# The rotor block's first two angle products moved in beside the gated block's last token sums

## The chip, the cores and the metric

The kernel runs on one core of one Trainium2 chip. The metric is the device time of one execution in microseconds, median of several. Three runs of the kernel before gave 814.88 us in the median (814.73 to 819.56).

## The reference, cut to what matters

Three blocks follow one another; the change lies where the second hands over to the third.

```python
x = attn(...)                       # (4, 768, 384): recurrent delta-rule attention
# gated block
h = np.maximum(x @ w_in, 0.0)       # u, v = halves of 512 columns
v_n = (v - mu) / np.sqrt(var + 1e-06)
v_s = np.einsum('ts,bsd->btd', w_spatial, v_n) + b_spatial[None, :, None]
x = (u * v_s) @ w_out
# rotor block
theta = x @ w_theta
zr, zi = x * np.cos(theta), x * np.sin(theta)
y = np.einsum('ts,bsd->btd', w_tok_r, zr) + np.einsum('ts,bsd->btd', w_tok_i, zi)
u = x + y
out = u + np.maximum(u @ w_ch, 0.0)
```

## The kernel before, in words

Every step is a task with a priority, the engines that can do it and the tiles it reads and writes (`Plan.add`, L152). While the program is built, a list scheduler (`Plan.run`, L237) takes the tasks one by one: for an engine, the ready task of the lowest priority number. The order in which it takes them is the fixed order of each engine's queue on the chip; a queue does not overtake. SP's queue issues all the DMAs.

A float32 product is made from three products of split operands (high·high, high·low, low·high), 128 rows at a time; `split` (L892) makes the two halves with a cast (ScalarE or VectorE) and a subtraction (VectorE or GpSimd).

The gated block, per batch b of 4, for each of 6 tiles of 128 tokens: `m_T` loads x transposed, `m_V` makes v and its layer norm, `m_U` makes u. Then six token sums `m_S` (L1058), 36 matmuls of 256 columns each; VectorE evicts each sum (L1069), multiplies it by u (L1072), and SP stores it. Those of the last batch have the priorities 1090 to 1095.

The rotor block, for 24 tiles (b, i): `X2` (L1227, 12 matmuls) is the product with w_out, evicted to tile x; `T2` (L1238) transposes it, with three evictions (xh, xl, x2T); `TH` (L1257, 9 matmuls) is the product with w_theta, followed by range reduction (ni, two steps of rr, a clamp), Sin, Abs, Sin of the rest, two products with x, and two splits into z. `Y` (L1285) adds the tile's part of the token sums, 36 matmuls into six PSUM banks y that are held for the whole batch: 18 with w_tok_r and z from the cosine, 18 with w_tok_i and z from the sine. After the sixth tile, `U2` and `O` finish the batch. The order that the priorities give is: X2 and T2 of tiles 0 and 1 at 1092.5 (XP, L54), TH of tiles 0 and 1 at 2004 and 2005, and then for each n: X2 and T2 of tile n+2 (2010 + 10n), Y of tile n (2013 + 10n), TH of tile n+2 (2013.5 + 10n).

PSUM: X2, T2, TH, the gated block's products and O share two banks m (`r_m`, L520). The six banks y are free from the end of the attention on.

SBUF: pools open and close. `ta` (L1150) opens p2a and the banks y once the attention is done. `tb` (L1160) closes the gated block's pools pm and wi and opens p2 once every task of the gated block is done, but for its last stores. In p2 lie all tiles of TH behind its product (ni, rr, sn, cs, z), the token weights of tiles 1 to 5, and the four buffers cvm3 (L1171) through which these weights are loaded from DRAM (L1179) before they are split. w_tok_i goes into the ring w3 (`r_wsp`, L899) that holds the gated block's token weights, a place at a time as those are done with. TH's matmuls wait for tb too.

Of the kernel before, what the change touches and what calls it, by code (L numbers as in the profile page):

```python
# [23 lines left out]
DM = H * D  # L24
# [5 lines left out]
TG = 256  # L30
# [20 lines left out]
THD = 1.5  # L51
LOADLAT = 2900
M3 = 4
XP = 1092.5  # L54
PMP = .5
PER = 6
HAMW = 4096 / 1.2
# [64 lines left out]
        return self.pools[self.pool].tile(self.shape, self.dtype, tag=self.tag, name=self.tag, bufs=self.bufs)  # L122


class Task:
    __slots__ = ("opts", "fn", "deps", "prio", "extra", "crit", "users", "left", "eng", "start", "end", "allocs", "uid", "big", "act", "credit", "order", "banks", "port", "part", "mode")

# [10 lines left out]
class Plan:  # L138
# [13 lines left out]
    def add(self, opts, fn, reads=(), writes=(), prio=0.0, extra=0.0, crit=False, after=(), big=False, act=0.292,  # L152
            port=True, part=0, mode=1):
        t = Task()


        t.port, t.part, t.mode = port, part, 0 if big else mode
        t.big, t.act, t.credit = big, 0.98 if big else act, 0.0
        t.opts, t.fn, t.prio, t.extra, t.crit = opts, fn, prio, extra, crit
        t.deps, t.users, t.allocs, t.eng, t.order = set(after), [], [], None, set()  # L160
        t.uid = len(self.tasks)
        t.banks = [b for b in reads if b.psum or b.ring is not None and b.ring.pool[:2] == "ps"]
        for b in reads:
            t.deps.update(b.writers)
            b.readers.append(t)
        for w in writes:
            b, part = w if isinstance(w, tuple) else (w, False)
            if not part:
                t.deps.update(b.readers)
                t.deps.update(b.writers)  # L170
            if b.first is None:
                b.first = t
                if b.ring is not None:
                    t.allocs.append(b)
            elif b.first is not t:
                t.order.add(b.first)
            b.writers.append(t)
        t.deps.discard(t)
        self.tasks.append(t)
        return t  # L180
# [234 lines left out]
def kernel(  # L415
# [34 lines left out]
    def ring(pl, tag, shape, dtype=F32, bufs=1):  # L450
        return Ring(pools, pl, shape, dtype, tag, bufs)
# [19 lines left out]
    def o_dve(n):  # L471
        return [("DVE", d_dve(n))]
# [21 lines left out]

    pool("const")
    pool("w3")
    pool("wi")
    pool("pm")
    pool("dram", space=bass.MemoryType.DRAM)
# [410 lines left out]
    r_wsr = Ring(pools, "w3", [128, HALF], F32, "gt", 2)  # L910
    r_gt = ring("w3", "gt", [128, 2, TG], F32, 2)
    r_wsr.items = r_gt.items
    r_xTh = ring("pm", "xTh", [128, KX, TG], F32R, 2)
    r_xTl = ring("pm", "xTl", [128, KX, TG], F32R, 2)
    r_uT = ring("pm", "uT", [128, KF, TG], F32, 3)
    r_hv = ring("pm", "hv", [128, DF], F32, HVN)
    r_st = ring("pm", "st", [128, 6], F32, 2)
# [195 lines left out]
                m_S(b, h3, fp, pr)  # L1113
                pr += 1

    r_bgr = ring("pm", "bgr", [128, BGW, 2], I32, 2)
    r_bgm = ring("pm", "bgm", [128, BGW], F32, 2)
    wdram = {}

    bg0 = [marks[BG0]]  # L1120
# [78 lines left out]
    r_x2T = ring("p2a", "x2T", [128, KX, S], F32, 2)  # L1199
    r_xh = ring("p2a", "xh", [128, KX, 128], F32R, 2)  # L1200
    r_xl = ring("p2a", "xl", [128, KX, 128], F32R, 2)
    r_ni = ring("p2", "ni", [128, DM], I32, 1)
    r_rr = ring("p2", "rr", [128, DM], F32, 2)
    r_sn = ring("p2", "sn", [128, DM], F32, 2)
    r_cs = ring("p2", "cs", [128, DM], F32, 2)
    r_z = [ring("p2", f"z{i}", [128, DM], F32R, 2) for i in range(4)]
    r_uf = ring("p2", "uf", [128, HALF], F32, 8)
    r_uh = ring("p2", "uh", [128, HALF], F32R, 4)
    r_ul = ring("p2", "ul", [128, HALF], F32R, 4)
    r_hp = ring("p2", "hpi", [128, 1], F32, 1)  # L1210
    hpi = r_hp.new()
    P.add([("POOL", 100.0)], lambda e: nc.gpsimd.memset(hpi.t, TWO_PI / 4), [], [hpi], 1900.0, port=False)
    sw = ring("p2a", "sw", [128, 1], F32, 1).new()
    P.add([("POOL", 100.0)], lambda e: nc.gpsimd.memset(sw.t, 0.0), [], [sw], 900.0, port=False)
    P.add([("ACT", 1500.0)], lambda e: act(sw.t, sw.t, ACTF.Sin), [], [sw], 903.0, after=sqrts)
# [3 lines left out]
    def load_g(b, h3, pr):  # L1219
        gh, gl = r_gh.new(), r_gl.new()  # L1220
        g_b[b, h3] = (gh, gl)
        for f in range(KF // 2):
            raw, gd = r_gr.new(), gdram[b][f][h3]
            P.add(dma(262144), lambda e, raw=raw, gd=gd: nc.sync.dma_start(out=raw.t, in_=gd.t), [gd], [raw], pr, extra=LOADLAT)
            split(raw, lambda raw=raw: raw.t, 2 * TG, gh, lambda f=f: gh.t[:, 2 * f:2 * f + 2], gl, lambda f=f: gl.t[:, 2 * f:2 * f + 2], pr)

    def X2(b, i, pr):  # L1227
        h3, o = i // 2, (i % 2) * 128
        if i % 2 == 0:
            load_g(b, h3, pr - 40 if pr >= 2000 else 903.0)  # L1230
        gh, gl = g_b[b, h3]
        ps, x2 = r_m.new(), r_x2.new()
        x2_b[b, i] = x2
        gr = [lambda f=f: (gh.t[:, f, o:o + 128], gl.t[:, f, o:o + 128], wo_h[f].t, wo_l[f].t) for f in range(KF)]
        mm_tasks(ps, lambda: ps.t[:, 0:DM], gr, DM, [[gh, gl, wo_h[f], wo_l[f]] for f in range(KF)], pr)
        P.add(o_cpp(DM), lambda e: copy(e, x2.t, ps.t[:, 0:DM]), [ps], [x2], pr, port=False)

    def T2(b, i, pr):  # L1238
        if i == 0:
            x2T_b[b] = [r_x2T.new()]  # L1240
        x2, ps, xT = x2_b[b, i], r_m.new(), x2T_b[b][0]
        xh, xl = xhl[b, i] = r_xh.new(), r_xl.new()
        v3 = (lambda: ps.t[:, 0:384].rearrange("p (k t) -> p k t", k=KX))

        def f(e):
            for kk in range(KX):
                nc.tensor.transpose(v3()[:, kk, :], x2.t[:, kk * 128:(kk + 1) * 128], ident.t)

        t = P.add(o_pe(245), f, [x2, ident], [ps, xh, xl], pr, act=0.95, mode=0)
        t.order.add(mfifo[-1])  # L1250
        mfifo.append(t)
        P.add([("ACT", d_actp(384))], lambda e: copy(e, xh.t, v3()), [ps], [xh], pr)
        P.add(o_dve(384), lambda e: nc.vector.tensor_tensor(out=xl.t, in0=v3(), in1=xh.t.bitcast(F32), op=ALU.subtract),
              [ps, xh], [xl], pr, port=False)
        P.add(o_cpp(384), lambda e: copy(e, xT.t[:, :, i * 128:(i + 1) * 128], v3()), [ps], [(xT, True)], pr, port=False)

    def TH(b, i, pr):  # L1257
        xh, xl = xhl[b, i]
        x2, ps = x2_b[b, i], r_m.new()
        gr = [lambda kk=kk: (xh.t[:, kk], xl.t[:, kk], wt_h[kk].t, wt_l[kk].t) for kk in range(KX)]  # L1260
        n1 = len(P.tasks)
        mm_tasks(ps, lambda: ps.t[:, 0:DM], gr, DM, [[xh, xl, wt_h[kk], wt_l[kk]] for kk in range(KX)], pr)
        for t in P.tasks[n1:]:
            t.deps.add(tb)
        ni, rr, sn, cs = r_ni.new(), r_rr.new(), r_sn.new(), r_cs.new()
        th = (lambda: ps.t[:, 0:DM])
        P.add(o_dve(DM), lambda e: nc.vector.tensor_scalar(out=ni.t, in0=th(), scalar1=1.0 / TWO_PI, scalar2=None, op0=ALU.mult),  # L1267
              [ps], [ni], pr, port=False)
        P.add(o_dve(DM), lambda e: nc.vector.scalar_tensor_tensor(out=rr.t, in0=ni.t, scalar=-C1, in1=th(), op0=ALU.mult, op1=ALU.add),  # L1269
              [ps, ni], [rr], pr, port=False)  # L1270
        P.add(o_dve(DM), lambda e: nc.vector.scalar_tensor_tensor(out=rr.t, in0=ni.t, scalar=-C2, in1=rr.t, op0=ALU.mult, op1=ALU.add),
              [ni], [rr], pr)
        P.add([("DVE", d_dve2(DM)), ("POOL", 1456.0)],
              lambda e: eng[e].tensor_scalar(out=rr.t, in0=rr.t, scalar1=PI_F, scalar2=-PI_F, op0=ALU.min, op1=ALU.max),
              [], [rr], pr)
        P.add([("ACT", d_acts(DM))], lambda e: act(sn.t, rr.t, ACTF.Sin), [rr], [sn], pr)
        P.add([("ACT", d_acts(DM))], lambda e: act(rr.t, rr.t, ACTF.Abs), [], [rr], pr)
        P.add([("ACT", d_acts(DM) + 93)], lambda e: act(cs.t, rr.t, ACTF.Sin, bias=hpi.t, scale=-1.0), [rr, hpi], [cs], pr)
        z = z_b[b, i] = [r.new() for r in r_z]
        for q, src in ((0, cs), (2, sn)):  # L1280
            P.add(o_tts(DM), lambda e, src=src: eng[e].tensor_tensor(out=src.t, in0=x2.t, in1=src.t, op=ALU.mult),
                  [x2], [src], pr)
            split(src, lambda src=src: src.t, DM, z[q], lambda q=q: z[q].t, z[q + 1], lambda q=q: z[q + 1].t, pr, part=False)

    def Y(b, i, pr):  # L1285
        z = z_b[b, i]
        for h3 in range(2):
            for q, (wh, wl) in ((0, (wr_h, wr_l)), (2, (wm_h, wm_l))):
                for d in range(KX):
                    if i == 0 and q == 0:  # L1290
                        y_b[b, d, h3] = r_y2[d][h3].new()
                    y = y_b[b, d, h3]
                    t0, t1 = h3 * HALF, (h3 + 1) * HALF
                    d0, d1 = d * 128, (d + 1) * 128
                    gr = [lambda q=q, wh=wh, wl=wl, t0=t0, t1=t1, d0=d0, d1=d1:
                          (z[q].t[:, d0:d1], z[q + 1].t[:, d0:d1], wh[i].t[:, t0:t1], wl[i].t[:, t0:t1])]
                    mm_tasks(y, lambda y=y: y.t, gr, HALF, [z[q], z[q + 1], wh[i], wl[i]], pr,
                             start=(i == 0 and q == 0), stop=(i == NT - 1 and q == 2))
# [27 lines left out]
    T2(*seq[0], XP + 0.1)  # L1326
    X2(*seq[1], XP + 0.2)
    T2(*seq[1], XP + 0.3)
    TH(*seq[0], pr + 4)
    TH(*seq[1], pr + 5)  # L1330
    for n, (b, i) in enumerate(seq):
        pr += 10
        if n + 2 < len(seq):
# [70 lines left out]
```

## Time and profile before

| | us |
|---|---|
| median of three runs | 814.88 (814.73 to 819.56) |
| profiled execution, device time | 812.64 |
| span of that execution, first to last instruction | 810.9 |
| TensorE busy in it | 750.0 |

The times quoted from the trace are microseconds from the span's start in the profiled execution. TensorE's matmuls are pipelined: the duration shown of one is longer than the distance to the next. The granted clock is a share of 2.4 GHz.

### The profile page before, as it was taken

Reading aid. Unit: us, or ns where it says so; the run is one execution under the profiler, and the core shown is the slowest. Engines: PE = TensorE matmul, PEld = TensorE weight load, DVE = VectorE, ACT = ScalarE, POOL = GpSimd, SP = SyncE. Lnnn points to the kernel's source line nnn. Section 1 sums busy time; section 2 is a strip of 40 time slices with the busy share of each in tenths; the row PEclk is TensorE's granted clock in tenths of the full one; section 3 lists DMA queues with packets and bytes.
Section 4 is the critical chain, followed back from the end, with each engine's and each line's share of the span. In section 5 each row is a group of like instructions: output and inputs, shape, how many; then the busy total and the mean of one; then the engine's idle time right before and its main releaser. Section 6 shows DMA issues by size and latency. Waiting matters only on the chain.

```text
span 810.9 us, 21951 instructions
## 1 busy us (share of the span) xinstructions
PE 750.0 (92%) x8904; PEld 685.8 (85%) x8904; DVE 623.9 (77%) x1537; ACT 342.5 (42%) x766; POOL 159.0 (20%) x178
## 2 busy tenths in 40 slices
PE   5389879989999989999999999889999999999998
PEld 5377658778987767888879999889999999999997
DVE  5989998999998999999775573787565575556545
ACT  4636326536444454534653351354333342333321
POOL 2026612543122241302011000131111111111100
PEclk9999989999999989999999999989999999999999
DMA  7626625454577887487884601451010011002001
GB/s 226 210 62 187 175 79 149 128 165 135 176 233 211 236 231 216 147 234 245 214 253 130 211 2 40 133 151 41 20 72 27 27 37 62 25 24 75 1 1 59
DMA packets 84997, 102.43 MB, mean 126 GB/s; under 512 B 8992, under 2 KB 65568, under 8 KB 84896
## 3 DMA queue, kind: packets, MB, share of 16 engines
q1 hardware_dynamic: 84896, 101.03, 42.1%
q8 instruction: 70, 1.15, 0.6%
q14 instruction: 31, 0.25, 0.1%
HBM read 74.38 MB, written 22.41 MB: 119 GB/s over the span
## 4 chain that ended last, share of the span: by engine, by line
PE 61%; DVE 26%; DMA 5%; issue 4%; ACT 2%; SPq 1%; POOL 1%; POOLq 0%; DVEq 0%; ACTq 0%
PE m L961 30%; PE y L961 19%; DVE un L721 5%; DVE tmp L709 5%; PE mg L486 2%; PE gp L651 2%; PE ru L832 1%; DVE kq L779 1%; PE py L860 1%; DVE un L687 1%; DVE bgm L886 1%; PE ru L821 1%; DMA kg<-in_kqT_dram 1%; PE s L848 1%; DVE GX L662 1%
## 5 line engine op out<-in xcount | busy, mean ns | idle before, releaser
L961 PE MATMUL m<-w,vh 128*128 128x256 f32 x576 | 110.3, 291 | 0.7 <-ACT uT L454 0.7
L961 PEld LDWEIGHTS m<-w,vh 128*128 128x128 f32 x576 | 89.0, 191 | 4.2 <-ACT uT L454 1.1
L961 PE MATMUL y<-wr,z 128*128 128x384 f32 x432 | 88.1, 343 | 0.0
L961 PE MATMUL y<-w,z 128*128 128x384 f32 x432 | 84.6, 339 | 0.0
L961 PE MATMUL m<-w,vl 128*128 128x256 f32 x288 | 81.5, 283 | 0.8 <-POOL vl L895 0.5
L961 PEld LDWEIGHTS y<-wr,z 128*128 128x128 f32 x432 | 77.3, 191 | 0.0
L961 PEld LDWEIGHTS y<-w,z 128*128 128x128 f32 x432 | 75.6, 188 | 0.0
L721 DVE TENSOR_TENSOR un<-un,tmp 128x30 f32<-128x30 f32 (+21 forms) x209 | 70.2, 348 | 1.1
L709 DVE TENSOR_TENSOR tmp<-un 128x30 f32<-128x30 f32 (+21 forms) x209 | 67.9, 337 | 1.2
L1267 DVE TENSOR_SCALAR ni<-m 128x384 int32<-128x384 f32 x24 | 13.3, 556 | 58.8 <-PE m L961 58.8
L961 PEld LDWEIGHTS m<-w,vl 128*128 128x128 f32 x288 | 54.9, 191 | 1.2 <-POOL vl L895 0.7
L961 PE MATMUL m<-wo,gh 128*128 128x384 f32 x192 | 48.9, 335 | 1.6 <-DVE rr L1269 1.6
L961 PE MATMUL m<-xTh,wih 128*128 128x256 f32 x144 | 46.3, 322 | 0.0
L454 ACT ACTIVATE W<-ru 64x192 f32<-64x192 f32 x88 | 28.5, 324 | 41.4 <-PE ru L833 40.1
L454 ACT ACTIVATE x<-m 128x384 f32<-128x384 f32 x15 | 7.3, 488 | 87.5 <-PE m L961 87.5
L629 POOL TENSOR_TENSOR gm<-mask,ng 128x256 f32<-128x256 f32 x53 | 36.4, 690 | 38.8 <-DVE pp L672 17.0
L797 POOL TENSOR_TENSOR vk<-vk,ng 128x384 f32<-128x384 f32 x25 | 23.7, 946 | 95.9 <-DMA vk<-in_vkn_dram 47.0
L486 PE MATMUL mg<-ident 128*128 128x128 f32 x231 | 39.6, 310 | 3.0 <-ACT GX L454 1.4
L832 PEld LDWEIGHTS ru<-rt,GX 64*64 64x64 f32 x384 | 26.2, 136 | 18.6 <-DVE rt L825 14.7
L832 PE MATMUL ru<-rt,GX 64*64 64x48 f32 x384 | 32.2, 224 | 10.0 <-DVE rt L825 9.4
L961 PE MATMUL m<-xTl,wih 128*128 128x256 f32 x144 | 40.6, 282 | 0.0
L961 PE MATMUL m<-xTh,wil 128*128 128x256 f32 x144 | 40.5, 281 | 0.0
(192 smaller groups left out, 2090.6 us busy)
## 6 DMA issues: line engine op xcount, KB each, us to landing
kq<-in_kqT_dram SPq DMA_DIRECT2D x96, 128.0 KB, 3.9
vk<-in_vkn_dram SPq DMA_DIRECT2D x48, 192.0 KB, 3.9
kg<-in_kqT_dram SPq DMA_DIRECT2D x32, 256.0 KB, 3.5
gd<-gt SPq DMA_DIRECT2D x24, 256.0 KB, 2.5
graw<-gd SPq DMA_DIRECT2D x24, 256.0 KB, 2.8
k<-in_vkn_dram SPq DMA_DIRECT2D x24, 192.0 KB, 3.2
xd<-xs SPq DMA_DIRECT2D x48, 96.0 KB, 3.2
xr<-xd SPq DMA_DIRECT2D x24, 192.0 KB, 3.5
```

The source lines that it names most:

```text
L454: nc.scalar.activation(out=out, in_=in_, func=func, **kw)
L486: nc.tensor.transpose(MGt[:, 256:384], ident.t, ident.t)
L629: eng[e].tensor_tensor(out=gm.t, in0=mask.t.unsqueeze(1).to_broadcast([128, HP, CH]), in1=ng_b[r].t[:, j, 1].unsqueeze(2).to_broadcast([12 ...
L651: mm(out=pv()[o:o + 64, hp, :], lhsT=kh, rhs=kg.t[i:i + D, :, hp, :] if fused else kh, start=True, stop=True)
L662: nc.vector.scalar_tensor_tensor(out=GXt[1][:, u0 + hp], in0=GXt[1][:, u0 + hp], scalar=ng_b[1].t[:, j, 1, hp:hp + 1], in1=mask.t, op0=ALU ...
L687: nc.vector.transpose(out=un.t, in_=gx[:, :, 0:32].rearrange("p u t -> p t u"))
L709: eng[e].tensor_tensor(out=t3, in0=un.t[:, k:k + 1, 0:k].to_broadcast([128, m, k]), in1=un.t[:, t0:32:st, k:k + 1].to_broadcast([128, m, k ...
L721: eng[e].tensor_tensor(out=un.t[:, t0:32:st, 0:k], in0=un.t[:, t0:32:st, 0:k], in1=t3, op=ALU.add)
L797: lambda e: eng[e].tensor_tensor(out=vk.t, in0=vk.t, in1=ng_b[r].t[:, j].unsqueeze(3).to_broadcast([128, 2, HP, D]), op=ALU.mult), [ng_b[r ...
L832: mm(out=pu.t[64:128, hp, :], lhsT=gx[64:128, u, :], rhs=rt.t[64:128, hp, :], start=True, stop=True)
L961: mm(out=view(), lhsT=a, rhs=c, start=(start and q == 0 and s_ == 0), stop=(stop and q == tot - 1 and s_ == 2))
L1267: P.add(o_dve(DM), lambda e: nc.vector.tensor_scalar(out=ni.t, in0=th(), scalar1=1.0 / TWO_PI, scalar2=None, op0=ALU.mult), [ps], [ni], pr ...
```

## The change

It makes TH of tiles 0 and 1 independent of tb and gives it an early priority.

- A new pool pz, which is never closed, takes four rings out of pm: xTh and xTl (the transposed x of the gated block) and bgr and bgm (buffers in which weights were converted during the attention). TH's tiles become later users of these places (`again`): rr takes bgm's; sn and cs are the two halves of bgr's; the four z are halves of xTh's and xTl's. ni lies on sn. There are two of each, as before (ni had one). p2's rings for them are gone.
- X2, T2 and TH of tiles 0 and 1 write into the six banks y, which are empty then (`bank`), in place of m.
- Their TH no longer waits for tb. Its priorities are 1092.5 and 1093.0 (TP) in place of 2004 and 2005; X2 and T2 move from 1092.5 to 1091.5 (XP).
- The constant hpi lies in p2a and is written early.
- Y of tile 0 does its 18 cosine matmuls first and then its 18 sine matmuls; before, the two alternated in nines.

```diff
-XP = 1092.5
+XP = 1091.5
+TP = (1092.5, 1093.0)
...
+    pool("pz")
...
-    r_xTh = ring("pm", "xTh", [128, KX, TG], F32R, 2)
-    r_xTl = ring("pm", "xTl", [128, KX, TG], F32R, 2)
+    r_xTh = ring("pz", "xTh", [128, KX, TG], F32R, 2)
+    r_xTl = ring("pz", "xTl", [128, KX, TG], F32R, 2)
...
-    r_bgr = ring("pm", "bgr", [128, BGW, 2], I32, 2)
-    r_bgm = ring("pm", "bgm", [128, BGW], F32, 2)
+    r_bgr = ring("pz", "bgr", [128, BGW, 2], I32, 2)
+    r_bgm = ring("pz", "bgm", [128, BGW], F32, 2)
...
-    r_ni = ring("p2", "ni", [128, DM], I32, 1)
-    r_rr = ring("p2", "rr", [128, DM], F32, 2)
-    r_sn = ring("p2", "sn", [128, DM], F32, 2)
-    r_cs = ring("p2", "cs", [128, DM], F32, 2)
-    r_z = [ring("p2", f"z{i}", [128, DM], F32R, 2) for i in range(4)]
+
+    def again(r, shape, dtype):
+        n = Ring(pools, r.pool, shape, dtype, r.tag, r.bufs)
+        n.items = r.items
+        return n
+
+    r_rr = again(r_bgm, [128, DM], F32)
+    r_sc = again(r_bgr, [128, 2, DM], F32)
+    r_zc, r_zs = again(r_xTh, [128, 2, DM], F32R), again(r_xTl, [128, 2, DM], F32R)
...
+    def bank(b, i, k):
+
+        return r_m.new() if b or i > 1 else r_y2[k][i].new()
+
...
-        ps, x2 = r_m.new(), r_x2.new()
+        ps, x2 = bank(b, i, 0), r_x2.new()
...
-        x2, ps, xT = x2_b[b, i], r_m.new(), x2T_b[b][0]
+        x2, ps, xT = x2_b[b, i], bank(b, i, 1), x2T_b[b][0]
...
-        x2, ps = x2_b[b, i], r_m.new()
+        x2, ps = x2_b[b, i], bank(b, i, 2)
...
-        for t in P.tasks[n1:]:
-            t.deps.add(tb)
-        ni, rr, sn, cs = r_ni.new(), r_rr.new(), r_sn.new(), r_cs.new()
+        if b or i > 1:
+            for t in P.tasks[n1:]:
+                t.deps.add(tb)
+        rr, sc = r_rr.new(), r_sc.new()
+        sn, cs = Half(sc, 0), Half(sc, 1)
+        ni = sn
...
-        z = z_b[b, i] = [r.new() for r in r_z]
+        z = z_b[b, i] = [Half(w, q) for w in (r_zc.new(), r_zs.new()) for q in range(2)]
...
-        for h3 in range(2):
-            for q, (wh, wl) in ((0, (wr_h, wr_l)), (2, (wm_h, wm_l))):
+        hq = [(h3, q) for h3 in range(2) for q in (0, 2)]
+        for h3, q in sorted(hq, key=lambda x: x[::-1]) if (b, i) == (0, 0) else hq:
+            for wh, wl in ((wm_h, wm_l) if q else (wr_h, wr_l),):
...
-    TH(*seq[0], pr + 4)
-    TH(*seq[1], pr + 5)
+    TH(*seq[0], TP[0])
+    TH(*seq[1], TP[1])
```

## Rows read from the trace of the kernel before

**Rows 1.** The page's head: the span and the instructions in it

```profile
span 810.9 us, 21951 instructions
```

**Rows 2.** Waits of TensorE from 440 us on, the longest: total, times, longest one

```profile
PE m L961 <- ACT xh L454: 2.6, 1, 2.6
PE m L1247 <- ACT x L454: 2.0, 1, 2.0
PE m L961 <- DVE rr L1269: 1.6, 1, 1.6
```

**Rows 3.** Windows: length, busy PE, PEld, DVE, ACT, POOL, then granted clock, DMA, GB/s

```profile
487.14:517.98 30.84, 30.84 (x247) 30.84 (x248) 12.01 (x20) 4.73 (x10) 0.00 (x0) 1.00 0.17 61
517.98:542.56 24.58, 18.39 (x92) 17.42 (x91) 20.70 (x35) 12.37 (x27) 7.21 (x7) 0.86 0.51 155
534.00:535.00 1.00, 1.00 (x4) 1.00 (x4) 1.00 (x3) 0.88 (x2) 0.00 (x0) 0.50 0.46 163
535.00:536.00 1.00, 1.00 (x7) 1.00 (x7) 0.79 (x3) 0.53 (x1) 0.00 (x0) 0.92 0.45 106
650.00:700.00 50.00, 50.00 (x293) 49.81 (x292) 31.23 (x59) 17.61 (x36) 6.05 (x5) 1.00 0.14 46
```

**Rows 4.** Timeline of TensorE: start, duration, operation, count, and the idle time before

```profile
517.98 0.52 PE L961 MATMUL m<-wt,xh 128*128 128x384 f32 x2
530.38 1.01 PE L961 MATMUL m<-wt,xh 128*128 128x384 f32 x2 [2.64 <-ACT xh L454]
532.47 2.96 PE L961 MATMUL y<-wr,z 128*128 128x384 f32 x9
540.48 0.51 PE L961 MATMUL m<-wo,gh 128*128 128x384 f32 x2
542.56 1.75 PE L961 MATMUL y<-wr,z 128*128 128x384 f32 x9
552.86 1.22 PE L961 MATMUL y<-wr,z 128*128 128x384 f32 x6
```

**Rows 5.** Timelines of VectorE: TH's first and last step, tile 0 and a later tile

```profile
521.29 0.55 DVE L1267 TENSOR_SCALAR ni<-m 128x384 int32<-128x384 f32 x1
530.84 0.78 DVE L895 TENSOR_TENSOR z<-cs,z 128x384 fp32r<-128x384 f32 x1
...
550.98 0.56 DVE L1267 TENSOR_SCALAR ni<-m 128x384 int32<-128x384 f32 x1 [0.31 <-PE m L961]
557.21 0.56 DVE L895 TENSOR_TENSOR z<-cs,z 128x384 fp32r<-128x384 f32 x1 [0.59 <-ACT z L454]
```

**Rows 6.** Timelines of SP, ScalarE, GpSimd and VectorE: token weights, and a load of gd

```profile
520.04 0.87 SPq L1179 DMA_DIRECT2D cvm<-wdr  x2
522.63 0.53 ACT L454 ACTIVATE wr<-cvm 128x384 fp32r<-128x384 f32 x1 [1.49 <-DMA cvm<-wdr]
526.81 2.37 POOL L895 TENSOR_TENSOR w<-cvm,w 128x384 fp32r<-128x384 f32 x2
535.24 0.55 DVE L895 TENSOR_TENSOR w<-cvm,w 128x384 fp32r<-128x384 f32 x1
544.51 0.92 SPq L1224 DMA_DIRECT2D graw<-gd  x2
516.81 1.03 DVE L895 TENSOR_TENSOR w<-cvm,w 128x384 fp32r<-128x384 f32 x2 [0.20 <-ACT w L454]
```

**Rows 7.** Timelines of TensorE, VectorE and ScalarE ahead of the sums

```profile
486.39 0.28 PE L961 MATMUL m<-xTh,wil 128*128 128x256 f32 x1
487.14 0.39 PE L961 MATMUL m<-w,vh 128*128 128x256 f32 x1 [0.47 <-ACT uT L454]
458.79 0.56 DVE L895 TENSOR_TENSOR wt<-cvm,wt 128x384 fp32r<-128x384 f32 x1 [0.96 <-ACT wt L454]
436.94 0.33 SPq L1129 DMA_DIRECT2D wdc<-bgm  x1
484.40 1.28 ACT L454 ACT_TABLE_LOAD   x1
```

More of the change, by code (lines that the diff above doesn't have):

```diff
@@ L122, in make, with __init__ @@
         return self.pools[self.pool].tile(self.shape, self.dtype, tag=self.tag, name=self.tag, bufs=self.bufs)
+class Half(Buf):
+    def __init__(self, whole, i):
+        self.whole, self.i = whole, i
+        super().__init__()
+    t = property(lambda self: self.whole.t[:, self.i], lambda self, x: None)
 class Task:
@@ L177, in add @@
             b.writers.append(t)
+        for x in [*reads, *writes]:
+            o = getattr(x[0] if isinstance(x, tuple) else x, "whole", None)
+            if o is not None:
+                if o.first is None:
+                    o.first = t
+                    t.allocs.append(o)
+                elif o.first is not t:
+                    t.order.add(o.first)
+                o.readers.append(t)
         t.deps.discard(t)
@@ L1209 @@
     r_ul = ring("p2", "ul", [128, HALF], F32R, 4)
-    r_hp = ring("p2", "hpi", [128, 1], F32, 1)
+    r_hp = ring("p2a", "hpi", [128, 1], F32, 1)
     hpi = r_hp.new()
-    P.add([("POOL", 100.0)], lambda e: nc.gpsimd.memset(hpi.t, TWO_PI / 4), [], [hpi], 1900.0, port=False)
+    P.add([("POOL", 100.0)], lambda e: nc.gpsimd.memset(hpi.t, TWO_PI / 4), [], [hpi], 900.0, port=False)
     sw = ring("p2a", "sw", [128, 1], F32, 1).new()
@@ L1249, in T2 @@
         t = P.add(o_pe(245), f, [x2, ident], [ps, xh, xl], pr, act=0.95, mode=0)
-        t.order.add(mfifo[-1])
-        mfifo.append(t)
+        if ps.ring is r_m:
+            if mfifo:
+                t.order.add(mfifo[-1])
+            mfifo.append(t)
         P.add([("ACT", d_actp(384))], lambda e: copy(e, xh.t, v3()), [ps], [xh], pr)
@@ L1262, in TH @@
         mm_tasks(ps, lambda: ps.t[:, 0:DM], gr, DM, [[xh, xl, wt_h[kk], wt_l[kk]] for kk in range(KX)], pr)
-        for t in P.tasks[n1:]:
-            t.deps.add(tb)
-        ni, rr, sn, cs = r_ni.new(), r_rr.new(), r_sn.new(), r_cs.new()
+        if b or i > 1:
[4 more added lines that the diff above has]
+        ni = sn
         th = (lambda: ps.t[:, 0:DM])
-        P.add(o_dve(DM), lambda e: nc.vector.tensor_scalar(out=ni.t, in0=th(), scalar1=1.0 / TWO_PI, scalar2=None, op0=ALU.mult),
+        P.add(o_dve(DM), lambda e: nc.vector.tensor_scalar(out=ni.t.bitcast(I32), in0=th(), scalar1=1.0 / TWO_PI, scalar2=None, op0=ALU.mult),
               [ps], [ni], pr, port=False)
-        P.add(o_dve(DM), lambda e: nc.vector.scalar_tensor_tensor(out=rr.t, in0=ni.t, scalar=-C1, in1=th(), op0=ALU.mult, op1=ALU.add),
+        P.add(o_dve(DM), lambda e: nc.vector.scalar_tensor_tensor(out=rr.t, in0=ni.t.bitcast(I32), scalar=-C1, in1=th(), op0=ALU.mult, op1=ALU.add),
               [ps, ni], [rr], pr, port=False)
-        P.add(o_dve(DM), lambda e: nc.vector.scalar_tensor_tensor(out=rr.t, in0=ni.t, scalar=-C2, in1=rr.t, op0=ALU.mult, op1=ALU.add),
+        P.add(o_dve(DM), lambda e: nc.vector.scalar_tensor_tensor(out=rr.t, in0=ni.t.bitcast(I32), scalar=-C2, in1=rr.t, op0=ALU.mult, op1=ALU.add),
               [ni], [rr], pr)
```

## The prediction

> **What bounds the kernel now.** The page's head gives the span of the profiled execution [rows 1]; its device time, 812.64 us, is 1.74 us more, and the median of the runs, 814.88 us, is 2.24 us above that. I work the sum out in the trace and take it from the median.
>
> The list of waits from 440 us on comes first [rows 2]. TensorE, busy nearly everywhere else, waits there three times for more than a microsecond: 2.6, 2.0 and 1.6 us, 6.2 us together, all between the last token sum of the gated block and the first Y. The reader is to see who ends them: the eviction of T2, that of X2, and a step of TH's range reduction on VectorE that sets a bank m free. Then the windows [rows 3]: through the sums TensorE is busy for 30.84 of 30.84 us, from their end to Y of tile 1 for 18.39 of 24.58 us, and from 650 to 700 us for all of it. So TensorE bounds both blocks, and only the handover between them does not keep it busy. In that stretch the granted clock falls as well: the mean is 0.86, and windows of 1 us show 0.50, the lower level of 1.2 GHz, until it rises within 535 to 536 us (0.92, so at about 535.16), after the idle stretch and some 4.8 us of matmuls. Last the timeline [rows 4]: TH of tiles 0 and 1 runs at 517.98 us, right after the sums, but Y of tile 0 only at 532.47 us, and its neighbour shows why: TH's own chain for tile 0, ni to the last half of z, starts at 521.29 us and ends at 531.62 us [rows 5]. VectorE, ScalarE and GpSimd make the angles of two tiles then, with the first token weights beside them, and TensorE has little else.
>
> **What the stall is worth.** Y of tile 1 starts at 542.56 us and Y of tile 2 at 552.86 us [rows 4]: a round of one X2, T2, Y and TH at full clock takes 10.30 us. From 540.48 to 542.56 us the 12 matmuls of one X2 take 2.08 us, 0.173 us each. Between 517.98 us and Y of tile 1 TensorE does one round's worth (X2 and T2 of tile 2, Y of tile 0, TH of tile 2), TH of tiles 0 and 1 (18 matmuls, 3.12 us) and X2 of tile 3 (2.08 us): 15.50 us. It takes 542.56 - 517.98 = 24.58 us. The difference, 9.08 us, is what the change can remove. It has three parts: 24.58 - 18.39 = 6.19 us idle [rows 3]; 4.78 us busy at half clock, from 530.38 to 535.16 us, half of it lost, 2.39 us; and 0.5 us for the ends of the matmuls ahead of three gaps (0.33 us shown of one against a distance of 0.173).
>
> **The change, step by step.**
>
> *TH of tiles 0 and 1, moved.* By the priorities TensorE does two sums, X2 and T2 of both tiles, a sum, TH of tile 0, a sum, TH of tile 1 (1093.0 stands equal with a sum made earlier, which goes first), two sums. A sum takes (30.84 - 2 x 2.08 - 2 x 0.42) / 6 = 4.31 us, T2's 0.42 being the round less its 57 other matmuls. From 487.14 us on this puts TH of tile 0 at 505.1 to 506.7 us, that of tile 1 at 511.0 to 512.5 us and the end of the sums at 521.10 us, 3.12 us later than now. The TensorE work is moved, none is added. TH's chain took 6.8 us for a later tile (550.98 to 557.77 us) and 10.3 us in the crowded handover [rows 5]; so z of tile 0 is there between 513.7 and 517.2 us, z of tile 1 between 519.5 and 523.0 us. Needed are they at 521.1 us at the earliest and at about 533.5 us. What hides the chains are the sums: in their 30.84 us VectorE is busy 12.01, ScalarE 4.73, GpSimd 0.00 us [rows 3]. Without this cover they would cost what they cost now. Behind TH's steps in VectorE's queue stand the evictions of the sums; a bank is wanted again one sum later, 4.3 us, so a step of 0.55 us in front costs nothing.
>
> *Places and banks.* bgm's last store is issued at 436.94 us; xTh's last reader starts at 486.39 us [rows 7]. Both are done with before 505 us, so rings of two add no wait. The empty banks take X2, T2 and TH out of the rotation of m; the sums keep both. The last Sin table load is at 484.40 us [rows 7], ahead of every Sin: no more of them. hpi is a memset: nothing.
>
> *Y's order.* Same matmuls. The cosine half comes first since w_tok_i of tile 0 waits for a place in w3: its split ended at 517.84 us, beside the last sum [rows 6], and ends at 520.96 us if it moves along; the sine half starts 18 matmuls after Y does, at 524.2 us at the earliest. Cost nothing.
>
> *After the sums.* 521.10 us, then X2 and T2 of tile 2, Y of tile 0, TH of tile 2 and X2 of tile 3, 12.38 us: Y of tile 1 at 533.48 us. What is late next are the token weights of tile 1. They are loaded into p2, which still opens only behind the last sum's evictions, so 3.12 us later: now the first loads go out at 520.04 us and the last split ends at 529.18 us [rows 6]. With the same queues that is 532.3 us, 1.2 us ahead of its use, though TH's chains of two tiles no longer stand beside them. Tile 2's weights, at 535.79 us now, come at 538.9 us for 543.8 us. TH and X2 issue no DMA; the loads of gd behind X2 of tile 1 go out earlier, into a stretch in which DMA is at 0.17 [rows 3].
>
> *Ahead of the sums* TensorE stands from 486.51 to 487.14 us, since ScalarE is late with the last evictions into m [rows 7]. X2 of tile 0, its operands ready (the last split of wt is at 458.79 us), no longer needs m and can fill this: between 0 and 0.63 us gained. I take nothing, since small new waits stand against it, and keep both ends.
>
> The sum: 814.88 - 9.08 = 805.8 us; the span would be 801.8 us.
>
> *The half clock.* The profile shows one execution's 4.78 us at 1.2 GHz. The Trainium skill, "TensorE: Matmul & The Clock Gate", Part 1, says that how many matmuls run slow around such a transition differs between runs of one kernel, as the chip's looking at the engine is not tied to the kernel's start. By the row the half clock is worth 2.39 us; by the rule it may be anything from nothing up in the runs that are timed, and without it the sum is 808.2 us.
>
> **The rivals.**
>
> *Part is given back at Y of tile 1.* If the splits of tile 1's weights are pushed back as far as those of tile 2 were (538.9 us against 533.5), TensorE waits 5.4 us and the gain is 3.7 us: 811.2 us. For it: the 1.2 us of slack, and VectorE near full in the stretch. Against it: the two chains that filled VectorE there are gone.
>
> *The half clock is no part of the timed runs:* 814.88 - 6.69 = 808.2 us. Against it: two of the three runs agree within 0.15 us, and all are above the profiled one.
>
> *The other side: SP's queue.* A load of gd waits for its buffer until X2 of tile 3 is done (544.51 us now, 1.95 us after that end) [rows 4, 6]. If such a load came to stand in front of tile 1's weights, these would go out at 533.48 + 1.95 + 0.92 = 536.4 us and be split 9.14 us later, at 545.5 us: Y of tile 1 would start 2.9 us later than now, and an idle stretch of 12 us would bring the half clock back, 2.4 us: 820.2 us. From 542.56 us on it is slower than before. Against it: the load stands behind nearly all token weights now.
>
> *No effect:* TH still waits for something at the end of the sums, and the handover stays: 814.9 us. I found no such reader of its places or banks.
>
> **How the numbers follow.** The forecast, a gain of 8.2 to 10, has 0.66; part given back 0.17; the half clock outside 0.08; SP's queue 0.03; no effect 0.06. About 1% (8.15 us) can be told from no change. Faster by more: 0.64, nearly all of the forecast; slower by more: 0.02, the SP queue with a bit on top; within: 0.34. The range goes from 804.4 us, with the gap filled and a longer half clock in the timed runs, to 809.0 us, which takes in the half clock and about half of the part given back.
>
> **What would show it.** The three waits [rows 2] gone and none over 1 us in their place; clock 1.00 from 487 us on; ni of tile 0 at about 507 us; Y of tile 0 within 3 us of the last sum; Y of tile 1 about 9 us earlier, at 533.5 us. Wrong would be: a TensorE wait for wr or w at Y of tile 1, a wait of the sums for gt's eviction behind ni or rr, or a second pair of table loads.

## The result and the profile after

| | before | after |
|---|---|---|
| median of 15 runs each, us | 818.98 (811.86 to 839.65) | 808.91 (803.54 to 812.55) |
| ratio after / before, 95% interval | | 0.9884 [0.9861, 0.9908] |
| profiled execution: device time, us | 812.64 | 808.91 |
| its span, us | 810.9 | 807.1 |

The change makes the kernel faster by 1.2% (0.9 to 1.4%). Ratios, here and below, leave out runs over 1.5% above the fastest of their kernel, of before those of 831.03 and 839.65 us, without which its median is 818.40 us. The forecast ratio, 805.8 / 814.88, is 0.9889. The time is another matter: put on the 818.98 us of the 15 runs, the ratio gives 809.5 us, 0.5 us above the range; the median itself, 808.91 us, is 3.1 us above the forecast and only 0.1 us inside the range. Of the three runs that the forecast started from, two, their median among them, are the second and third lowest of the 15.

The two spans differ by only 3.8 us, less than the handover alone gained. The last layer norm of the gated block comes 6.3 us later in the profile of after, and the attention before it varies by up to 4.7 us between profiles of one kernel (last experiments). So I count from the start of the last Sqrt, near the end of that layer norm: 484.18 us in the profile of before, 490.48 us in that of after, and a second profile of each.

| from the last Sqrt, us | before | before again | after | after again |
|---|---|---|---|---|
| first matmul behind the sums, forecast 36.92 | 33.80 | 33.78 | 36.20 | 36.20 |
| Y of tile 0 | 48.29 | 48.27 | 38.29 | 38.29 |
| Y of tile 1, forecast 49.30 | 58.38 | 58.24 | 48.58 | 48.58 |
| from there to the last matmul | 264.54 | 264.52 | 263.97 | 263.46 |
| end of the span | 326.72 | 326.55 | 316.62 | 316.05 |

The windows follow, with the columns of [rows 3]: in before, from the last Sqrt to the end of the sums; in after the same, now with X2, T2 and TH of two tiles among the sums, then from their end to Y of tile 1, then the rest.

```profile
484.18:517.98 33.80, 33.33 (x268) 33.13 (x268) 14.49 (x28) 7.66 (x15) 0.00 (x0) 1.00 0.16 55
...
490.48:526.68 36.20, 36.20 (x286) 36.17 (x285) 22.74 (x46) 12.05 (x23) 0.00 (x0) 1.00 0.14 49
526.68:539.06 12.38, 12.38 (x74) 12.35 (x73) 8.01 (x16) 6.79 (x14) 0.00 (x0) 1.00 0.64 205
539.10:803.00 263.90, 263.35 (x1536) 261.59 (x1535) 164.85 (x307) 94.17 (x193) 33.69 (x29) 1.00 0.13 43
```

TensorE is busy through the handover, which lasts 12.38 us instead of 24.58, and the granted clock (the first number behind POOL's) stays at 1.00. VectorE's work on the first angles has gone to the stretch ahead: 22.74 us there against 14.49. The list of TensorE's waits from 480 us on, which held the three of [rows 2], has one line left, at 550.94 us, behind Y of tile 1:

```profile
PE m L1276 <- DVE bgm L1303: 0.4, 1, 0.4
```

The timeline of TensorE (start, duration, operation, count) shows where the moved work went: X2 of tile 0 half at 492.82 and half at 502.50 us, TH of tile 0 at 510.60 us, the end of the sums at 526.68 us, Y of tile 0 with its cosine half and its sine half, and Y of tile 1. It answers to [rows 4].

```profile
492.82 0.52 PE L982 MATMUL y<-wo,gh 128*128 128x384 f32 x2
...
502.50 0.52 PE L982 MATMUL y<-wo,gh 128*128 128x384 f32 x2
...
510.60 0.52 PE L982 MATMUL y<-wt,xh 128*128 128x384 f32 x2
...
526.68 0.52 PE L982 MATMUL m<-wo,gh 128*128 128x384 f32 x2
...
528.77 1.23 PE L982 MATMUL y<-wr,xTh 128*128 128x384 f32 x6
...
532.28 3.30 PE L982 MATMUL y<-w,xTl 128*128 128x384 f32 x18
...
539.06 1.73 PE L982 MATMUL y<-wr,xTh 128*128 128x384 f32 x9
```

VectorE's timeline has TH of tile 0 from its first step to its last split of z, between two sums' evictions (L1090), where [rows 5] had it behind the sums, and the last split of a weight of tile 1, which [rows 6] has on GpSimd, at 526.81 us. Names are those of the places now: bgr holds ni, xTl and xTh hold z.

```profile
512.37 0.56 DVE L1301 TENSOR_SCALAR bgr<-y 128x384 int32<-128x384 f32 x1
...
517.03 0.69 DVE L1090 TENSOR_TENSOR gt<-m,bsp_sb 128x512 f32<-128x512 f32 x1
517.70 0.56 DVE L916 TENSOR_TENSOR xTh<-bgr,xTh 128x384 fp32r<-128x384 f32 x1
...
535.03 1.05 DVE L916 TENSOR_TENSOR w<-cvm,w 128x384 fp32r<-128x384 f32 x2 [2.11 <-ACT w L474]
```

z of tile 0 is there at 518.3 us, 10.5 us before its use. The weight of tile 1 is split by 536.1 us, 3.0 us before Y of tile 1.

### The profile page after: what moved, and what is told of

Its sections match the earlier page's. It is cut to its first block, busy times and chain, and to the rows that moved or that the text cites. A ratio compares the mean times of both kernels' runs of the same rounds, so it can differ in the third digit from the quotient of the medians.

```text
span 807.1 us, 21948 instructions
## 1 busy us (share of the span) xinstructions
PE 749.4 (93%) x8904; PEld 684.7 (85%) x8904; DVE 622.8 (77%) x1543; ACT 342.3 (42%) x763; POOL 155.9 (19%) x175
## 4 chain that ended last, share of the span: by engine, by line
PE 60%; DVE 23%; DMA 6%; issue 4%; ACT 4%; SPq 2%; POOL 1%; POOLq 0%; DVEq 0%; ACTq 0%
PE m L982 29%; PE y L982 19%; DVE un L742 5%; DVE tmp L730 4%; PE mg L506 2%; PE gp L672 2%; DMA bgr<-in_w_r_dram 2%; ACT GX L474 2%; PE py L881 1%; PE ru L853 1%; DVE kq L800 1%; PE ru L842 1%; DVE GX L683 1%; DVE bgm L907 1%; PE s L869 1%
## 5 line engine op out<-in xcount | busy, mean ns | idle before, releaser
L982 PE MATMUL y<-wr,xTh 128*128 128x384 f32 x432 | 86.2, 337 | 0.0
L982 PE MATMUL y<-w,xTl 128*128 128x384 f32 x432 | 83.9, 336 | 0.0
L982 PEld LDWEIGHTS y<-wr,xTh 128*128 128x128 f32 x432 | 75.3, 188 | 0.0
L982 PEld LDWEIGHTS y<-w,xTl 128*128 128x128 f32 x432 | 75.1, 188 | 0.0
L730 DVE TENSOR_TENSOR tmp<-un 128x30 f32<-128x30 f32 (+21 forms) x209 | 65.2, 322 | 1.2
L1301 DVE TENSOR_SCALAR bgr<-m 128x384 int32<-128x384 f32 x22 | 12.2, 555 | 55.1 <-PE m L982 55.1
L982 PE MATMUL m<-wo,gh 128*128 128x384 f32 x176 | 44.7, 334 | 0.0
L672 PE MATMUL gp<-kg 48*64 48x128 f32 x512 | 37.5, 290 | 3.2 <-DVE pp L693 1.8
```

The lines of the kernel that those rows point to most:

```text
L672: mm(out=pv()[o:o + 64, hp, :], lhsT=kh, rhs=kg.t[i:i + D, :, hp, :] if fused else kh, start=True, stop=True)
L730: eng[e].tensor_tensor(out=t3, in0=un.t[:, k:k + 1, 0:k].to_broadcast([128, m, k]), in1=un.t[:, t0:32:st, k:k + 1].to_broadcast([128, m, k ...
L982: mm(out=view(), lhsT=a, rhs=c, start=(start and q == 0 and s_ == 0), stop=(stop and q == tot - 1 and s_ == 2))
L1301: P.add(o_dve(DM), lambda e: nc.vector.tensor_scalar(out=ni.t.bitcast(I32), in0=th(), scalar1=1.0 / TWO_PI, scalar2=None, op0=ALU.mult), [ ...
```

## The experiments

All experiments but the timed ones of the last part are one profile each, read from the trace and not by their time. In this section, handover is the time from the last Sqrt to Y of tile 1.

**The kernels once more.** A second profile of each gives the columns "again" above.

> The kernel before, profiled once more. Two stretches are read: the attention (start to the last layer norm's Sqrt, 484.2 us before and 490.5 us after the change, though the order of every queue is the same up to there) and the handover (from that Sqrt to Y of tile 1, 58.4 us before, 48.6 us after). Theory A, the attention varies from execution to execution: here it lies anywhere in some 480 to 500 us, and the handover is again 58.4 within 1 us. Theory B, the new places (pool pz) slow the attention down: here it is 484 us again within 1 us.

> The kernel after, profiled once more. Theory A: attention anywhere in 480 to 500 us, not tied to the kernel; handover again 48.6 us within 0.3 us, since nothing in it waits. Theory B: attention again at 490 us within 1 us, 6 us above that of the kernel before on the same chip.

Before again has the same three waits, 2.6, 2.0 and 1.6 us, and a clock of 0.86 from the end of the sums to Y of tile 1; after again has 48.58 us at Y of tile 1. The handover repeats within 0.14 us. The attention does not: the last Sqrt is at 486.85 and 489.55 us. Theory B's 484 us did not come again, but after again is within 1 us of its 490; these two profiles do not settle whether the new places slow the attention (see the last experiments).

**The places and banks alone, without the early angles.**

```diff
-TP = (1092.5, 1093.0)
+TP = (2004.0, 2005.0)
```

> All of the change but the early priority: TH of tiles 0 and 1 keeps the new places and the empty banks, but has its old priorities 2004 and 2005. Theory 1, the gain is TH's chain under the sums: the handover from the last Sqrt to Y of tile 1 is 56 to 58 us, at most the 0.6 us gap ahead of the sums and the 1.6 us wait for a bank m gained. Theory 2, the gain is the banks and places: 49 to 52 us.

The waits of TensorE in this kernel, and then its windows (from the last Sqrt to the end of the sums, from there to Y of tile 1):

```profile
PE m L982 <- ACT xh L474: 4.2, 1, 4.2
PE m L1276 <- ACT x L474: 1.7, 2, 1.1
```

```profile
489.20:522.20 33.00, 33.00 (x268) 32.97 (x267) 14.32 (x28) 7.67 (x15) 0.00 (x0) 1.00 0.16 57
522.20:545.10 22.90, 18.16 (x94) 17.15 (x93) 19.54 (x33) 11.51 (x25) 6.58 (x5) 0.85 0.48 151
```

Y of tile 1 stands at 55.84 us behind the Sqrt, just under the 56 to 58 us of theory 1, 2.5 us better than before and 7.3 us worse than after. The stretch behind the sums has its clock of 0.85 back and 4.7 us idle. (The longer of the two waits for x, 1.1 us, lies behind Y of tile 1.) Of the three waits of [rows 2] only the one for a bank m (1.6 us) is gone for good; with the filled gap ahead of the sums (0.63 us) that is nearly all of the 2.5. So the places and banks are there to let TH run early, and the early TH is worth most of the gain.

**Early angles for tile 0 only.**

```diff
-TP = (1092.5, 1093.0)
+TP = (1092.5, 2005.0)
```

> After the change, but only TH of tile 0 is early; that of tile 1 has its old priority 2005 and runs behind the last sum. Theory 1a, only tile 0's chain was on the path: tile 1's z is wanted 12.4 us later, which covers a chain of 6.8 to 10.3 us; the handover (last Sqrt to Y of tile 1) stays at 48.6 us within 0.5. Theory 1b, both are needed: a wait ahead of Y of tile 1 and 50 us or more, since X2, T2 and the weights want the same engines then.

Y of tile 1 is at 48.58 us, as in after, with one wait of 0.8 us later on. The chain of tile 0 is the one that TensorE waited for; that of tile 1 has Y of tile 0 (6.2 us) to hide behind.

**The clock by itself.** To the kernel before, transposes of no use are added in the idle stretches of the handover, so that TensorE does not rest.

```diff
...
+    for _ in range(15):
+        P.add(o_pe(246.0), dummy, [ident], [(fz, True)], 2900.0, act=0.95, mode=0, after=ends)
```

Each `dummy` is three 128x128 transposes into a free bank y, and `ends` are the matmuls of TH of tiles 0 and 1.

> The kernel before with 45 transposes of no use put into the three idle stretches of the handover (into a bank y that is empty then). It parts the 9.08 us of the stall into idle time and half clock. If the half clock is worth what the one profile says, the granted clock stays at 1.00 and the handover is 2.4 us shorter, about 56 us; if transposes don't hold the clock up, or it is no part of the usual run, it stays at 58.4 us; if they come in the way of the products, it is longer.

The window from the end of the sums to Y of tile 1, and then the longest group of the transposes on TensorE's timeline:

```profile
522.88:545.57 22.69, 21.39 (x137) 20.31 (x136) 19.65 (x33) 12.23 (x27) 8.22 (x8) 1.00 0.51 160
```

```profile
532.48 2.46 PE L1335 MATMUL y<-ident 128*128 128x128 f32 x21
```

The window is 22.69 us long where [rows 3] has 24.58. The granted clock stays at 1.00, and Y of tile 1 comes at 56.48 us, 1.8 to 1.9 us earlier than in the two profiles of before. The half clock's term, 2.39 us, is thus somewhat large, or the added work cost half a microsecond of it; the rest of the 9.8 us is idle time.

**X2, T2 and TH of tiles 0 and 1 in the banks m.**

```diff
-        return r_m.new() if b or i > 1 else r_y2[k][i].new()
+        return r_m.new()
```

> After the change, but X2, T2 and TH of tiles 0 and 1 write to the two banks m again in place of the empty banks y. My theory: the gap of 0.6 us ahead of the sums is not filled, otherwise nothing: handover 49.2 to 49.5 us. Rival: the sums wait for banks that T2's three evictions hold, 1 us or more at two places: 50.5 us or more.

TensorE's waits, and then from its timeline the first matmul behind the sums:

```profile
PE m L982 <- ACT uT L474: 0.5, 1, 0.5
PE m L1276 <- ACT x L474: 0.4, 1, 0.4
```

```profile
526.87 0.52 PE L982 MATMUL m<-wo,gh 128*128 128x384 f32 x2
```

The gap ahead of the sums is back, and 526.87 is 36.91 us behind this kernel's Sqrt (489.96 us), where the forecast, which had the gap left open, put 36.92. Against 36.20 us in after the empty banks buy 0.7 us here. Y of tile 1 comes at 49.90 us, 0.4 us later than the highest value expected; 0.37 us of that is a wait of T2 of tile 2 for x. The sums themselves did not wait for the evictions of TH.

**Y's order.** `for h3, q in hq:` in place of the sorted loop, so that Y of tile 0 alternates in nines as before.

> After the change, but Y of tile 0 alternates cosine and sine matmuls in nines as before. The split of w_tok_i for tile 0 ended 0.1 us after the last sum in the profile of after, 2 us ahead of Y: handover 48.6 us within 0.2. Rival: the sine half waits for that split at its new place, 1.6 us after Y's start: up to 1 us more.

Y of tile 1 is at 48.60 us: the order costs and gains nothing, as taken.

**The buffers of the token weights.** M3, the number of buffers cvm3, is 4 in both kernels.

```diff
-M3 = 4
+M3 = 2
```

> After the change with two buffers in place of four for the loads of the token weights. It measures how near the weights are to being the next bound. Theory: a unit of four halves then takes two loads one after the other, some 8 us, and TensorE's round is 10.3 us; tile 1's last split comes about 10 to 11 us after the last sum, Y of tile 1 wants it at 12.4 us: handover 48.6 us within 0.5, and no wait over 1 us later. Rival, the weights are at the edge already: waits at Y of tiles 1 to 5, 2 us or more at the first.

```diff
-M3 = 4
+M3 = 1
```

> After the change with one buffer for the loads of the token weights: each half of a unit waits for the split of the one before. Theory, the weights are the next bound but well covered: a half takes some 4 us, a unit 16 against a round of 10.3 us, so TensorE waits ahead of Y of tiles 1 to 5, 3 to 6 us each, 15 to 25 us in all from the last Sqrt to the end. Rival, the pool's opening sets it and not the buffers: 5 us or less.

With two buffers nothing changes: 48.57 us, no TensorE wait behind the Sqrt. With one, Y of tile 1 is still on time (48.58 us), but the stretch behind it takes 284.77 us, 21.3 us more than in after again. The four largest groups of waits of that kernel from 530 us on:

```profile
PE y L982 <- ACT w L474: 4.5, 4, 1.2
PE m L982 <- ACT xh L474: 3.1, 4, 1.1
PE y L982 <- ACT wr L474: 2.3, 2, 1.2
PE m L982 <- DVE xl L1284: 2.2, 5, 0.6
```

The 15 to 25 us that the theory gave for the whole hold, its 3 to 6 us ahead of each Y do not: the waits come to 14.0 us, none above 1.2, and about half of that is not ahead of Y's matmuls. With one buffer the weights, and the evictions beside them, hold TensorE up behind Y of tile 1; with two or four they do not.

**The matmuls of Y behind the handover.** From Y of tile 1 to the last matmul, after is 0.6 to 1.1 us shorter than before. The groups of Y (count, busy us, mean ns) from 545.2 us on, first before, then after:

```profile
L961 PE MATMUL y<-wr,z 128*128 128x384 f32 x405 | 81.7, 340 | 0.0
```

```profile
L982 PE MATMUL y<-wr,xTh 128*128 128x384 f32 x396 | 79.2, 337 | 0.0
```

They take 3 ns less apiece by the profile. (The ends of matmuls are modelled in it; the length of the stretch is the firmer measure.) z now is one tile of two halves where it was four tiles, so I gave the kernel before that form, in p2 as it was:

```diff
-    r_z = [ring("p2", f"z{i}", [128, DM], F32R, 2) for i in range(4)]
+    r_z = [ring("p2", f"z{i}", [128, 2, DM], F32R, 2) for i in range(2)]
```

The lines of `split` and Y that name z follow suit; they are left out here.

> The kernel before, but the high and low halves of z lie side by side in one tile, as after the change, in p2 as before. It parts why the stretch from Y of tile 1 to the last matmul was 264.5 us in the kernels with z in p2 and 263.5 us with z in the places of xTh and xTl, with the same matmuls: layout, then 263.5; place, then 264.5 us. Handover 58.4 us either way.

The stretch stays at 264.58 us and the mean at 340 ns: the form is not the cause. In the kernel with late angles, whose z lie where they lie in after, the mean is 337 ns and the stretch, less its wait of 1.1 us, 263.6 us. That points to the new places, of z or of rr, sn and cs, which moved along with it; which of them it is, and by which property, stays open.

The same profile shows the half clock differently. Its windows in the handover:

```profile
534.00:535.00 1.00, 1.00 (x4) 1.00 (x4) 1.00 (x4) 1.00 (x4) 0.23 (x1) 0.50 0.00 0
535.00:536.00 1.00, 1.00 (x5) 1.00 (x5) 1.00 (x2) 0.40 (x1) 1.00 (x1) 0.62 0.08 16
```

Matmuls begin again at 532.92 us and the clock is up again within 535 to 536 us (0.62, so at about 535.76): 2.84 us at 1.2 GHz, not 4.78. Half of the difference is 0.97 us, and Y of tile 1 comes at 57.49 us, 0.75 to 0.9 us earlier than in before and than expected. Before again lies close to before: matmuls begin at 533.03 us, and the clock is up within 537 to 538 us (0.74, so at about 537.52), 4.49 us.

```profile
537.00:538.00 1.00, 1.00 (x6) 1.00 (x6) 1.00 (x4) 0.53 (x2) 0.00 (x0) 0.74 0.16 38
```

**Where the microseconds ahead of the handover come from.** The order of instructions up to the last Sqrt is the same in before and after on all engines, but for the early memset of hpi on GpSimd and a few neighbouring matmuls, which change places between the two profiles of before as well; yet the last Sqrt stands between 484.18 and 491.87 us over 14 profiles of kernels whose edits concern what follows it, and between 485.79 and 490.48 us over four of after alone. The mean is 489.3 us over the ten profiles with the new places and 486.7 us over the four without, so these profiles leave room for an attention that the change makes 2 to 3 us longer; the timed runs do not show it (see the next part). One step of the attention, from the 34th to the 35th of 44 updates of the state, takes 7.11 us in before and 7.5 to 11.6 in the others. The timeline of ScalarE in it, first before, then the kernel with Y in nines:

```profile
377.31 0.56 ACT L454 ACTIVATE bgm<-bgr 128x384 f32<-128x384 f32 x1 [2.40 <-DMA bgr<-in_w_r_dram]
377.90 0.38 ACT L454 ACTIVATE ct<-mg 32x256 f32<-32x256 f32 x1
```

```profile
382.53 0.55 ACT L474 ACTIVATE bgm<-bgr 128x384 f32<-128x384 f32 x1 [5.78 <-DMA bgr<-in_w_r_dram]
383.10 0.38 ACT L474 ACTIVATE ct<-mg 32x256 f32<-32x256 f32 x1
```

A conversion of a weight, of no hurry, stands in ScalarE's queue ahead of a step of the attention (ct), and ScalarE waits 3.4 us longer for its load here; ct's operand had been done since 379.65 us. My theory was that these loads make the spread. First the timed comparison of after was repeated beside a kernel in which the planner takes such loads as 1.5 us slower than it does, and so queues each conversion later; then both again in more rounds, with 3 us as well (3000 in place of 1500).

```diff
-                t.extra = dmaq + DMA_POST - t.end
+                t.extra = dmaq + DMA_POST - t.end + max(0.0, t.extra - LOADLAT)
...
-              extra=LOADLAT, after=after)
+              extra=LOADLAT + (1500 if after else 0), after=after)
```

> The kernel after once more, timed beside the kernel before and beside the next kernel on the same chip. Attention (start to the last Sqrt) anywhere in 484 to 495 us, handover 48.6 us; a ratio of about 0.988 to the kernel before.

> After the change; the planner counts 1.5 us more for the landing of the rotor weights' loads during the attention, so that their conversions stand later in ScalarE's and VectorE's queues. Theory A1, the attention's spread comes from these loads landing late ahead of in-order queues (5.8 us of ScalarE idle in one profile, 2.4 in another, at the same place): the waits of ScalarE on these loads fall to less than half and the attention is 3 us or more shorter than that of the kernel after in the same call, with less spread. Theory A2, the spread is in something else (the gram loads, VectorE, the clock): no change beyond 1 us, or a longer attention, as all the order moves.

> The kernel after, as the base of the next two: ratio 0.988 to the kernel before, runs spread over some 8 us.

> After with 1.5 us more allowed for the landing of the rotor weights' loads. Theory A1, ScalarE's waits on these loads make the spread: median 2 to 5 us below the kernel after of the same call, runs spread over half as much. Theory A2, the spread is elsewhere: median and spread within 1.5 us of those of the kernel after.

> After with 3 us more allowed. Theory A1: ScalarE's waits on these loads nearly gone (under 3 us), median at or below that of 1.5 us more. Theory A2: as the kernel after, or slower by what the later conversions hold back, since the two buffers of the loads are given back later.

| | ratio to before | median (all runs), us | ScalarE's waits for bgr up to the Sqrt, us |
|---|---|---|---|
| after, 3 rounds | 0.9867 [0.9815, 0.9919] | 805.12 (802.85 to 812.0) | |
| 1.5 us, 3 rounds | 0.9825 [0.9783, 0.9868] | 804.07 (800.47 to 807.16) | 5.8 |
| after, 5 rounds | 0.9873 [0.9834, 0.9911] | 806.48 (803.14 to 815.63) | 30.8 |
| 1.5 us, 5 rounds | 0.9830 [0.9789, 0.9871] | 804.97 (799.63 to 814.03) | 5.0 |
| 3 us, 5 rounds | 0.9914 [0.9883, 0.9945] | 810.2 (805.26 to 819.88) | 1.4 |

The waits go, from 17.8 us in the first profile of after and 30.8 in that of the five rounds to 5 and 1.4. The spread from the lowest to the highest run does not follow: in the five rounds it is 14.4 us with 1.5 us, 12.5 in after and 14.6 with 3 us. But that hangs on the highest run of each; without it, it is 5.8, 10.0 and 8.8 us, and in the three rounds 6.7 us with 1.5 us against 9.2. So few runs do not settle the spread, but three things speak against the theory. With 3 us the kernel is slower than with 1.5, with the fewest waits of all. The last Sqrt came 2.3 us later with 1.5 us than in after of the same rounds (488.10 against 485.79 us), where 3 us earlier were expected, and 3.2 us earlier the second time (485.45 against 488.60), one profile each. And the profile of after with 30.8 us of waits has its Sqrt 1.9 us ahead of the one with 17.8. Those waits are one place at which an execution loses time; that they make the spread is not shown. The first profile of after loses time elsewhere too: an instruction of VectorE that starts 0.2 us earlier than in before at 246 us starts 2.4 us later at 258 us. A window of it, beside the same window of before:

```profile
245.00:255.00 10.00, 10.00 (x169) 8.39 (x165) 8.54 (x18) 2.34 (x7) 3.10 (x3) 0.66 0.62 187
```

```profile
245.00:255.00 10.00, 9.98 (x183) 7.92 (x184) 8.89 (x21) 3.60 (x10) 1.56 (x2) 1.00 0.65 189
```

A clock of 0.66 against 1.00, and 169 matmuls against 183. Yet the mean clock does not order the profiles: from 20 to 480 us it is 0.96 in the profile of after with the earliest Sqrt (485.79 us) and 0.97 in the kernel with Y in nines, which has the latest (491.87 us). What sets this off in one execution and not in another stays open. Why 3 us is slower stays open too. The kernel with 1.5 us is the fastest that was run; its interval overlaps that of after, so these runs don't tell whether it is faster.

## Why the prediction was right or wrong

- **The level was wrong, and with it the time.** The step that failed is "I work the sum out in the trace and take it from the median": 814.88 us was the median of three runs that I took as firm because two agreed within 0.15 us. Over 15 runs it is 818.98, from 811.86 to 839.65. The profiled execution, 6.3 us below that median, had the shortest attention of these 14 profiles. The range of 4.6 us counted only what the change might do and left out that the level of three runs is itself uncertain by some 4 us: the same sum from 818.98 us gives 809.9 us, above the range. That the median, 808.91 us, still lies inside is luck: the gain was about 1 us larger than the sum, by the gap ahead of the sums and by Y's matmuls (below). Three values in the given table, 814.73 to 819.56, spanned 4.8 us; I read two of them as agreement and not the third as spread.
- **The stall and its price were right.** The sum for the handover was 9.08 us, and 0.63 us more if the gap ahead of the sums were filled: 9.71. Measured at Y of tile 1: 9.80 us (9.66 against before again). The stretch from the end of the sums to Y of tile 1 was put at 12.38 us and took 539.06 - 526.68 = 12.38. Kernel before with full clock and kernel after with late angles confirm its parts: idle time for the most part, the clock for 1.8 to 1.9 us.
- **The gap ahead of the sums was wrongly taken as nothing.** X2 of tile 0 fills it, since it needs no bank m; 0.7 us, as the kernel with banks m shows. I set small new waits against it; there was one of 0.4 us, in one of the two profiles, and behind Y of tile 1.
- **The half clock.** The term was 2.39 us by the row. Both profiles of before show about the same clock behind the sums, 0.86, and full clock was worth 1.8 to 1.9 us. The half clock was there in every profile of a kernel with that stall (before twice, late angles, z in two tiles), which speaks against the rival that it is no part of the timed runs (808.2 us). Its length was 4.78 and 4.49 us in before, and 2.84 us in the kernel with z in two tiles; it moved Y of tile 1 by 0.9 us at most. The Trainium skill, "TensorE: Matmul & The Clock Gate", Part 1, says that the number of slow matmuls around a transition differs between runs of one kernel. The two profiles of before agree with that, by 0.29 us only; the third is of another kernel and does not show it by itself.
- **The token weights.** The slack was put at 1.2 us and was 3.0: the splits came earlier in relation to Y than the old queues gave. The rival of 811.2 us fell with it; two buffers were enough.
- **SP's queue.** The load of graw went out at 541.83 us, behind the weights that Y of tile 1 needed. That rival found no place either.
- **Places, Y's order.** No wait for a place shows, and the order was worth 0.02 us.
- **Not in the sum:** the matmuls of Y behind the handover, 0.6 to 1.1 us. With these, 9.9 to 10.7 us are gained from the last Sqrt to the end of the span. The timed ratios (0.9884, 0.9867, 0.9873) say 9.5, 10.9 and 10.4 us, the first of them uncertain by 1.9 us: the timed runs show no cost of the change in the attention, and a small one stays open.

The share was forecast at 1.11% and measured at 1.16%; the sign holds, and "faster by over 1%" holds for the ratio, though its interval reaches down to 0.92%.

## What to carry to other kernels

When the bounding engine rests at a handover between two blocks, look for a chain of another engine's work whose operands were ready long before, and for what pinned it to the handover: here a pool that opened too late and two shared banks. Price it by what the bounding engine would do in the stretch at its steady pace; that held to 0.1 us once the gap ahead of the sums was counted, where a sum of waits (6.2 us) would have missed a third. Forecast a change of one per cent as a ratio, and give the time a range that holds the spread of the runs it starts from.

## What the runs showed of the hardware

- The kernel after varied by 4.7 us in its first 490 us from profile to profile, with no change of its instructions. Seen at single places, between before and others, were longer waits for a load, with urgent work held behind the waiting instruction in the same queue (2.40 us against 5.78), and stretches at a lower granted clock (0.66 against 1.00 over 10 us). Neither the sum of such waits nor the mean clock put the profiles in order.
- Transposes of no use kept the granted clock at 1.00 through a stretch in which the kernel before got 0.86.
- 128x384 matmuls of Y took 337 instead of 340 ns by the profile, and their stretch 0.6 to 1.1 us less, when z and TH's other tiles lay at other places in SBUF; the form of z's tile was not the reason.
